# The steps at which a kernel prepares the next batch's softmax, set anew: both transposes in step 10, the state's read in step 12

## The chip, the cores and the metric

One Trainium2 chip, one of its cores. The metric is the device time of one execution in microseconds (us), the median of several runs; one further execution was taken with the hardware profiler, and all rows below are from it.

## The reference

The attention-like front end reads 8 batches of 512 tokens (8 heads of width 64) against 32 state vectors per head, in both directions, and two feed-forward layers follow on all 8 x 544 rows:

```python
scores = scale * np.matmul(x, state.transpose(0, 1, 3, 2))      # softmax over the 32 states
xread = np.matmul(a, state)
scores2 = scale * np.matmul(state, x.transpose(0, 1, 3, 2))     # softmax over the 512 tokens
sread = np.matmul(a2, x)
...
h = x @ w_in;  r = np.maximum(h, 0.0);  x = (s * (r * r) + b) @ w_out
h = x @ w_in;  g = h * (1.0 / (1.0 + np.exp(-h)));  out = g @ w_out
```

## The kernel before

All matrix products are of 32-bit accuracy: each operand is split into a high and a low part, and three products (high x high, high x low, low x high) are summed. For the first layer the states are folded into the first weights beforehand (the tiles `G`), so that its left operand is the softmax itself (`at_h`, `at_l`, the tiles `xh` and `xl`).

The first layer runs block by block. Block i (i = 1 to 7) is batch i; block 0 was done in a start-up part, and a last block holds the state rows. A block has 16 steps f. In `run`, one step issues in this order: the second half of the activation of step f-1 (`finish`: `gh` on ScalarE, L613, then `gl` on VectorE, L614), six matmuls of the first product (`mm1_a`, L566) into one of two banks `ph`, the activation's first half (relu on ScalarE, L607, then a square with scale on VectorE, L608), twelve matmuls of the second product of step f-3 (`mm2_a`, L628, which read `gh` and `gl` of step f-3), and then the extras of step f:

```python
do(f, 0)
finish()
pend.append((i, f, act_a(mm1_a(f, k), width[k], i)))
do(f, 1)
...
flush(LAG)          # LAG = 3
...
do(f, 2)
```

Every engine works through its queue in the order in which this code issues. The extras, kept by `extra(bi)` in a table of (step, place), are:

- the softmax of batch i+1, in two halves p and q (`Half`), in blocks 1 to 6. `score` (step 1) is on TensorE. Then for each half, in the order of the list `names`: `tr`, `rd`, `nb` (VectorE), `ex` (exp, ScalarE, gives `e2` and its sums); `mx`, `sb` (L470, L476, VectorE), `en` (exp, L481, ScalarE); `n0`, `n1` (tiny) and `n2` (L494, VectorE: `e2` times the reciprocal of its sum); `s0` to `s2` (L511 to L521), `s3` (L525), `s4` (L531), all on VectorE; `tu` (L503: four 128x128 transposes of `e2` on TensorE into a bank of the pool "a", which has two), `pl` (ScalarE, pulls that bank to `a2`); `ah` (ScalarE) and `al` (VectorE, L232), which make the `xh` and `xl` of the next block;
- `read` (L390, 64 small matmuls that read `a2` of both halves) and `pull_read` (L398); `load_all` of `xn`, the batch's rows that the next block's `read` needs (four loads on SyncE's DMA queue, L364);
- `split_g`, which splits the folded weights of later steps (a ScalarE copy, L229, and a VectorE subtraction, L232);
- conversions of the 64-bit weights for later: one ScalarE operation (L189) and four VectorE bit operations (L197 to L211) for each tile, sums of tiles (L750), reorders on ScalarE (L229).

```python
def n2(self, dve=True):
    ... nc.vector.tensor_scalar(out=self.e2, in0=self.e2, scalar1=self.rs, ...)
def tu(self, at="a"):
    self.pt = bank(at, [P, 4, P])
    for t in range(4):
        nc.tensor.transpose(self.pt[:, t, :], self.e2[:, t * P:(t + 1) * P], ident)
```

Of the kernel before, what the change touches and what calls it, by code (L numbers as in the profile page):

```python
# [87 lines left out]
def fused_kernel(ctx: ExitStack, tc, xt, xn, sbd, sg, w1, w2, sv, bv, out):  # L88
# [573 lines left out]
    def run(blocks, pend):  # L662
# [10 lines left out]
        for i, k in enumerate(blocks):  # L673
            if i == 0:
                continue
            ops = extra(i)

            def do(f, when):
                for op in ops.get((f, when), ()):
                    op()  # L680

            for f in range(NF):
# [4 lines that stand above are left out]
                last = f == NF - 1 and i + 1 == len(blocks)  # L687
                if last:
                    finish()
                flush(LAG)  # L690
                if f == NF - 1 and not last:
                    prepare_a(blocks[i + 1])
                if last:
                    flush(0)
                do(f, 2)
# [632 lines left out]
    def last_block(add):  # L1328

        def give(*tags):
            add(f, 2, spare.extend, tags)

        splits = [(p, c) for p in RIGHT for c in range(2)]
        inputs[0] = Inputs(0)
        for f in range(NF):
            if f == 0:
                give("xt0", "xt1", "xn0", "xn1", "sbd",
                     "xh2", "xh3", "xl2", "xl3", *(f"v{i}" for i in range(24, 30)),  # L1340
                     *(f"xr{i}" for i in range(4)))
                for i in range(2):
                    add(f, 2, carve, f"raw{i}", 4)
                add(f, 2, inputs[0].load)
            if f >= 2:
                give(f"wh{f - 2}", f"wl{f - 2}")
            if f == 7:
                give(*(f"mid{i}" for i in range(4)))
                give(*(f"v{i}" for i in range(8, 16)))
            if f == 11:  # L1350
                give(*(f"v{i}" for i in range(8)))
            if f == 15:
                give(*(f"v{i}" for i in range(16, 24)))
            if 2 <= f < 4:
                for name in ("T1", "T2", "T3"):
                    add(f, 2, inputs[0].sum, name, f - 2)
            for i, what in ((f - 4, inputs[0].high), (f - 5, inputs[0].low)):
                if 0 <= i < len(splits) // 2:
                    for p, c in splits[2 * i:2 * i + 2]:
                        add(f, 2, what, p, c)  # L1360
            for i, what in ((f - 6, "load"), (f - 9, "high"), (f - 10, "low")):
                if i >= 0 and i % 2 == 0 and i // 2 < 5:
                    if what == "load":
                        quads[i // 2] = list(duos_in(i // 2))
                    for x in quads[i // 2]:
                        add(f, 2, getattr(x, what))
# [53 lines left out]
    def extra(bi):  # L1420
        k = order[bi]
        ops = {}

        def add(f, when, op, *args):
            ops.setdefault((f, when), []).append(lambda: op(*args))

        if bi < B - 1:

            halves = [Half(k + 1, j) for j in range(2)]
            add(1, 2, score, k + 1, halves)  # L1430
            add(1, 2, load_sbd, k + 2)
            add(2, 0, load_all, k + 2, xt)
            names = "tr rd nb ex mx sb en n0 n1 n2 s0 s1 s2 s3 s4 tu pl ah al"
            when = (
                (1, 1, 1, 1, 3, 3, 3, 3, 3, 4, 5, 5, 5, 6, 6, 6, 6, 7, 8),
                (2, 2, 2, 2, 7, 7, 7, 7, 7, 8, 9, 9, 9, 10, 10, 9, 10, 11, 12),
            )
            for h, fs in zip(halves, when):
                for f, name in zip(fs, names.split()):
                    add(f, 2, getattr(h, name))  # L1440
            add(11, 2, read, k + 1, halves)
            add(12, 0, load_all, k + 2, xn)
            add(12, 2, pull_read, k + 1, halves)
        def add_g(f0, fs, *g):
            for j in range(2):
                add(f0, 0, load_g, *g, j)
                add(fs[j], 2, split_g, *g, j)

        if bi == 1:
            add_g(0, (1, 2), 1, 1)  # L1450
            add(2, 0, load_all, 2, xn)
        if bi < B:

            for fg, (f0, *fs) in enumerate(((1, 4, 4), (3, 6, 7), (9, 12, 13), (11, 14, 15))):
                if fg < 2:
                    g = k, fg + 2
                elif k + 1 < B:
                    g = k + 1, fg - 2
                else:
                    continue  # L1460
                add_g(f0, fs, *g)
        for f in range(NF):
            for when in range(3):
                for op in later.pop((NF * bi + f, when), ()):
                    add(f, when, op)
        if bi == B - 1:
            for i, pair in enumerate(stream[:2]):
                add(5 + 3 * i, 0, load32, pair)
            for i in range(RING // 2):
                add(9 + 2 * i, 2, split_next)  # L1470
        if bi == B:
            for f in (0, 1, 4, 5):
                add(f, 2, split_next)
            last_block(add)
        return ops
# [79 lines left out]
```

## Time and profile before

| what | us |
|---|---|
| median of 3 runs (lowest to highest) | 1343.88 (1342.68 to 1344.85) |
| the profiled execution | 1343.82 |
| its span, first to last instruction | 1342.0 |
| TensorE busy | 1309.4 |
| VectorE busy | 993.8 |
| ScalarE busy | 741.1 |
| blocks 1 to 6, the stretch that the change touches | about 137 to 550 |

"Busy" of TensorE is the union of its matmuls; a matmul's end in the trace is modelled. In a row of a timeline the first number is the start in us from the span's start, the second the duration, and a bracket at the end gives how long the engine stood idle before it and which instruction ended that.

### The profile page before, as it was taken

Reading aid. Unit: us, or ns where it says so; the run is one execution under the profiler, and the core shown is the slowest. Engines: PE = TensorE matmul, PEld = TensorE weight load, DVE = VectorE, ACT = ScalarE, POOL = GpSimd, SP = SyncE. Lnnn points to the kernel's source line nnn. Section 1 sums busy time; section 2 is a strip of 40 time slices with the busy share of each in tenths; the row PEclk is TensorE's granted clock in tenths of the full one; section 3 lists DMA queues with packets and bytes.
Section 4 is the critical chain, followed back from the end, with each engine's and each line's share of the span. In section 5 each row is a group of like instructions: output and inputs, shape, how many; then the busy total and the mean of one; then the engine's idle time right before and its main releaser. Section 6 shows DMA issues by size and latency. Waiting matters only on the chain.

```text
span 1342.0 us, 20852 instructions
## 1 busy us (share of the span) xinstructions
PE 1309.4 (98%) x6928; PEld 1133.0 (84%) x6928; DVE 993.8 (74%) x1794; ACT 741.1 (55%) x1360; POOL 0.7 (0%) x7
## 2 busy tenths in 40 slices
PE   5999999999999999999999999999999999999997
PEld 3678778787787777888988888999998888899997
DVE  8899797879797979865867757575767765655654
ACT  7999554444454545544665645464666635353541
POOL 0000000000000000000000000000000000000000
PEclk9999999999999999999999999999999999999999
DMA  8888555554565545343748565657699886677583
GB/s 304 304 304 287 190 189 196 171 182 143 172 203 180 179 160 180 127 151 90 231 150 290 205 226 212 234 191 242 210 297 351 304 262 189 179 238 228 168 259 88
DMA packets 182925, 284.01 MB, mean 212 GB/s; under 512 B 25632, under 2 KB 99360, under 8 KB 182816
## 3 DMA queue, kind: packets, MB, share of 16 engines
q1 hardware_dynamic: 182016, 282.28, 63.5%
q8 instruction: 54, 0.88, 0.3%
q10 hardware_dynamic: 800, 0.39, 0.1%
q14 instruction: 55, 0.45, 0.1%
HBM read 166.72 MB, written 115.87 MB: 211 GB/s over the span
## 4 chain that ended last, share of the span: by engine, by line
PE 79%; DVE 9%; DMA 6%; ACT 3%; issue 2%; SPq 1%; ACTq 0%; DVEq 0%
PE bank L902 48%; PE o L628 18%; PE ph L566 10%; DMA raw<-w 3%; DVE r L608 1%; DVE v L232 1%; DVE gl L614 1%; PE bank L281 1%; DMA v<-gd 1%; ACT wf L189 1%; DVE wf L206 1%; ACT xr L229 1%; DMA gd<-xr 1%; DMA x<-o 1%; SPq L327 0%
## 5 line engine op out<-in xcount | busy, mean ns | idle before, releaser
L566 PE MATMUL ph<-xh,v 128*128 128x512 f32 (+1 forms) x640 | 207.2, 375 | 0.1
L628 PE MATMUL o<-gh,wh 128*128 128x512 f32 (+1 forms) x448 | 169.9, 379 | 0.0
L628 PE MATMUL o<-gl,wh 128*128 128x512 f32 (+1 forms) x448 | 169.7, 379 | 0.0
L628 PE MATMUL o<-gh,wl 128*128 128x512 f32 (+1 forms) x448 | 169.7, 379 | 0.0
L566 PEld LDWEIGHTS ph<-xh,v 128*128 128x128 f32 x640 | 117.9, 190 | 27.0 <-issue 5.0
L608 DVE SCALAR_TENSOR_TENSOR r<-r,s_sb 128x512 f32<-128x512 f32 (+1 forms) x128 | 91.4, 714 | 49.9 <-ACT r L607 49.7
L607 ACT ACTIVATE r<-ph 128x512 f32<-128x512 f32 (+1 forms) x128 | 72.0, 563 | 94.6 <-PE ph L566 92.1
L566 PE MATMUL ph<-xl,v 128*128 128x512 f32 (+1 forms) x320 | 118.5, 370 | 0.0
L613 ACT ACTIVATE gh<-r,b_sb 128x512 fp32r<-128x512 f32 (+1 forms) x96 | 66.5, 693 | 57.7 <-DVE r L608 57.5
L628 PEld LDWEIGHTS o<-gh,wh 128*128 128x128 f32 x448 | 84.8, 189 | 15.8
L628 PEld LDWEIGHTS o<-gh,wl 128*128 128x128 f32 x448 | 84.6, 189 | 15.9
L628 PEld LDWEIGHTS o<-gl,wh 128*128 128x128 f32 x448 | 84.6, 189 | 15.7
L902 PE MATMUL bank<-v,v 128*128 128x384 f32 (+1 forms) x316 | 96.2, 360 | 0.0
L614 DVE SCALAR_TENSOR_TENSOR gl<-r,b_sb,gh 128x512 fp32r<-128x512 f32 (+1 forms) x96 | 68.5, 713 | 15.4 <-ACT gh L613 15.4
L902 PE MATMUL bank<-wh,v 128*128 128x384 f32 (+1 forms) x230 | 76.6, 352 | 0.0
L628 PE MATMUL o<-v,wh 128*128 128x512 f32 (+1 forms) x256 | 75.2, 377 | 0.0
L566 PEld LDWEIGHTS ph<-xl,v 128*128 128x128 f32 x320 | 60.7, 190 | 9.3
L902 PEld LDWEIGHTS bank<-v,v 128*128 128x128 f32 x316 | 58.6, 188 | 5.8
L628 PEld LDWEIGHTS o<-v,wh 128*128 128x128 f32 x256 | 46.9, 188 | 9.2 <-DVE o L641 0.5
L211 DVE SCALAR_TENSOR_TENSOR wf<-raw,wf 128x512 uint32<-128x512 uint32 (+1 forms) x65 | 52.9, 814 | 2.0
L902 PE MATMUL bank<-wl,v 128*128 128x384 f32 (+1 forms) x153 | 52.9, 357 | 0.4 <-DVE wh L750 0.4
L206 DVE SCALAR_TENSOR_TENSOR wf<-raw,wf 128x512 uint32<-128x512 uint32 (+1 forms) x65 | 52.2, 803 | 0.2
(1066 smaller groups left out, 3179.2 us busy)
## 6 DMA issues: line engine op xcount, KB each, us to landing
raw<-w SPq DMA_DIRECT2D x80, 512.0 KB, 4.9
gd<-xr SPq DMA_DIRECT2D x48, 256.0 KB, 2.9
v<-gd SPq DMA_DIRECT2D x192, 64.0 KB, 2.2
go<-v SPq DMA_DIRECT2D x54, 192.0 KB, 2.1
go<-v SPq DMA_DIRECT2D x38, 256.0 KB, 2.3
v<-go SPq DMA_DIRECT2D x45, 192.0 KB, 3.3
v<-go SPq DMA_DIRECT2D x31, 256.0 KB, 4.7
go<-wl SPq DMA_DIRECT2D x35, 192.0 KB, 2.1
```

The source lines that it names most:

```text
L189: nc.scalar.activation(out=tf, in_=hi.bitcast(F32), func=AF.Abs)
L206: nc.vector.scalar_tensor_tensor(out=t, in0=lo, scalar=29, in1=t, op0=ALU.logical_shift_right, op1=ALU.bitwise_or,)
L211: nc.vector.scalar_tensor_tensor(out=t, in0=hi, scalar=0xC0000000, in1=t, op0=ALU.bitwise_and, op1=ALU.bitwise_or,)
L229: nc.scalar.activation(out=out, in_=x, func=AF.Copy)
L232: nc.vector.tensor_tensor(out=lo, in0=x, in1=hi.bitcast(F32), op=ALU.subtract)
L566: nc.tensor.matmul(ph[:, :n], a, x, start=j == 0 and i == 0, stop=j == last and i == 2)
L607: nc.scalar.activation(out=r, in_=ph[:, :n], func=AF.Relu)
L608: nc.vector.scalar_tensor_tensor(out=r, in0=r, scalar=s_sb, in1=r, op0=ALU.mult, op1=ALU.mult)
L613: nc.scalar.activation(out=gh, in_=r, func=AF.Identity, bias=b_sb)
L614: nc.vector.scalar_tensor_tensor(out=gl, in0=r, scalar=b_sb, in1=gh.bitcast(F32), op0=ALU.add, op1=ALU.subtract)
L628: nc.tensor.matmul(po[c][:, :n], a, x, start=f == 0 and i == 0, stop=f == NF - 1 and i == 2)
L902: nc.tensor.matmul(bank[:, :n], a, x, start=start and j == 0 and i == 0, stop=stop and j == last and i == 2, skip_group_check=True,)
```

## The change

In the table `when` of `extra`, each half has a row of 19 steps, one for each name of the list `names`. Half p's `s0` to `s4`, `ah`, `tu` and `pl` come later, half q's `mx`, `sb`, `en`, `n0`, `n1` come earlier (from step 7 to 5), and q's `tu` and `pl` one step later. `read`, `pull_read` and the `xn` loads move by one step. Nothing is added or removed.

```diff
             names = "tr rd nb ex mx sb en n0 n1 n2 s0 s1 s2 s3 s4 tu pl ah al"
             when = (
-                (1, 1, 1, 1, 3, 3, 3, 3, 3, 4, 5, 5, 5, 6, 6, 6, 6, 7, 8),
-                (2, 2, 2, 2, 7, 7, 7, 7, 7, 8, 9, 9, 9, 10, 10, 9, 10, 11, 12),
+                (1, 1, 1, 1, 3, 3, 3, 3, 3, 4, 6, 6, 6, 7, 7, 10, 11, 8, 8),
+                (2, 2, 2, 2, 5, 5, 5, 5, 5, 8, 9, 9, 9, 10, 10, 10, 11, 11, 12),
             )
...
-            add(11, 2, read, k + 1, halves)
-            add(12, 0, load_all, k + 2, xn)
-            add(12, 2, pull_read, k + 1, halves)
+            add(12, 2, read, k + 1, halves)
+            add(13, 0, load_all, k + 2, xn)
+            add(13, 2, pull_read, k + 1, halves)
```

TensorE, block 1, the end of step 6 and the start of step 7 (`mid_1719` is half p's `e2`; lines with - are of before, with + of the change):

```order
 L628 MATMUL o_1824<-gl_1809,wh_897 128x512
 L628 MATMUL o_1824<-gh_1808,wl_908 128x512
-L503 MATMUL bank<-ident,mid_1719 128x128 x4
 L566 MATMUL ph<-xh_1152,v_1722 128x512
 L566 MATMUL ph<-xl_1471,v_1722 128x512
```

The transposes of half p leave step 6 and nothing takes their place. Now the place that they go to, the end of step 10 of the same block (`mid_1787` is half q's `e2`):

```order
+L628 MATMUL o_1824<-gl_1962,wh_1207 128x512
+L628 MATMUL o_1824<-gh_1961,wl_1224 128x512
+L503 MATMUL bank<-ident,mid_1719 128x128 x4
 L503 MATMUL bank<-ident,mid_1787 128x128 x4
 L566 MATMUL ph<-xh_1152,v_1866 128x512
```

Both halves' transposes now stand in one place, behind the second product of step 7 (its `gh` and `gl` have the numbers 1961 and 1962); half q's stood there behind step 9's matmuls, one step earlier.

VectorE, block 1, from step 5's square (`r_1885`) on, before (`mid_1714` and `mid_1782` are the scores `sn` of p and q, `gl_1887` is `gl` of step 5):

```order
L608 SCALAR_TENSOR_TENSOR r_1885<-r_1885,s_sb 128x512
L511 TENSOR_REDUCE sm<-mid_1714 128x16
L516 TENSOR_SCALAR sm<-sm 128x16
L521 RECIPROCAL sm<-sm 128x16
L197 TENSOR_SCALAR wf_1792<-wf_1792 128x512
L201 TENSOR_SCALAR wf_1792<-wf_1792 128x512
L614 SCALAR_TENSOR_TENSOR gl_1887<-r_1885,b_sb,gh_1886 128x512
L608 SCALAR_TENSOR_TENSOR r_1917<-r_1917,s_sb 128x512
L525 TENSOR_TENSOR mid_1714<-mid_1714,sm 128x512
L531 STREAM_TRANSPOSE v_1935<-mid_1714 128x512
```

and from the same instruction on in the changed kernel:

```order
L608 SCALAR_TENSOR_TENSOR r_1885<-r_1885,s_sb 128x512
L470 TENSOR_REDUCE mx<-mid_1782 128x16
L476 TENSOR_TENSOR mid_1782<-mid_1782,mx 128x512
L485 TENSOR_SCALAR sum_1788<-sum_1788 128x1
L490 RECIPROCAL sum_1788<-sum_1788 128x1
L197 TENSOR_SCALAR wf_1792<-wf_1792 128x512
L201 TENSOR_SCALAR wf_1792<-wf_1792 128x512
L614 SCALAR_TENSOR_TENSOR gl_1887<-r_1885,b_sb,gh_1886 128x512
L608 SCALAR_TENSOR_TENSOR r_1919<-r_1919,s_sb 128x512
L511 TENSOR_REDUCE sm<-mid_1714 128x16
L516 TENSOR_SCALAR sm<-sm 128x16
L521 RECIPROCAL sm<-sm 128x16
```

Half q's four operations take the place of p's three, and p's move one step back each; from step 8 on both orders have had the same instructions.

ScalarE, block 1, from step 5's relu (`r_1885`) on, before:

```order
L607 ACTIVATE r_1885<-ph 128x512
L613 ACTIVATE gh_1886<-r_1885,b_sb 128x512
L607 ACTIVATE r_1917<-ph 128x512
L229 ACTIVATE mid_1942<-bank 128x512
L229 ACTIVATE v_1944<-v_1794 128x512
L189 ACTIVATE wf_1953<-raw_1836 128x1024
L613 ACTIVATE gh_1918<-r_1917,b_sb 128x512
L607 ACTIVATE r_1964<-ph 128x512
L229 ACTIVATE xh_1981<-v_1935 128x512
L481 ACTIVATE mid_1782<-mid_1782 128x512
L229 ACTIVATE v_1946<-v_1796 128x512
L613 ACTIVATE gh_1965<-r_1964,b_sb 128x512
```

and in the changed kernel:

```order
L607 ACTIVATE r_1885<-ph 128x512
L481 ACTIVATE mid_1782<-mid_1782 128x512
L613 ACTIVATE gh_1886<-r_1885,b_sb 128x512
L607 ACTIVATE r_1919<-ph 128x512
L229 ACTIVATE v_1940<-v_1794 128x512
L189 ACTIVATE wf_1949<-raw_1836 128x1024
L613 ACTIVATE gh_1920<-r_1919,b_sb 128x512
L607 ACTIVATE r_1960<-ph 128x512
L229 ACTIVATE v_1942<-v_1796 128x512
L613 ACTIVATE gh_1961<-r_1960,b_sb 128x512
```

Half q's exponential (L481) moves from behind step 7's relu to behind step 5's, and half p's pull (`mid_1942`) and `xh` leave these steps.

## Rows read from the trace of the kernel before

**Rows 1.** The page's first part: busy us, share, instructions.
```profile
PE 1309.4 (98%) x6928; PEld 1133.0 (84%) x6928; DVE 993.8 (74%) x1794; ACT 741.1 (55%) x1360; POOL 0.7 (0%) x7
```
**Rows 2.** Waits of TensorE from 137 to 641 us: us, times, longest.
```profile
PE bank L503 <- DVE mid L494: 8.5, 6, 2.7
```
**Rows 3.** Timeline of TensorE, the transposes of half q, blocks 1 to 6.
```profile
178.47 0.63 PE L503 MATMUL bank<-ident,mid 128*128 128x128 f32 x4 [0.72 <-DVE mid L494]
...
249.79 0.63 PE L503 MATMUL bank<-ident,mid 128*128 128x128 f32 x4 [2.38 <-DVE mid L494]
...
323.03 1.09 PE L503 MATMUL bank<-ident,mid 128*128 128x128 f32 x4 [2.67 <-DVE mid L494]
...
394.00 0.63 PE L503 MATMUL bank<-ident,mid 128*128 128x128 f32 x4 [0.56 <-DVE mid L494]
...
464.09 0.63 PE L503 MATMUL bank<-ident,mid 128*128 128x128 f32 x4 [1.02 <-DVE mid L494]
...
534.29 0.63 PE L503 MATMUL bank<-ident,mid 128*128 128x128 f32 x4 [1.12 <-DVE mid L494]
```
**Rows 4.** Timeline of TensorE: block 3, first matmuls of steps, half p's transposes.
```profile
303.39 0.39 PE L566 MATMUL ph<-xh,v 128*128 128x512 f32 x1
...
307.47 0.60 PE L503 MATMUL bank<-ident,mid 128*128 128x128 f32 x4
307.83 0.48 PE L566 MATMUL ph<-xh,v 128*128 128x512 f32 x1
...
312.04 0.39 PE L566 MATMUL ph<-xh,v 128*128 128x512 f32 x1
...
316.12 0.39 PE L566 MATMUL ph<-xh,v 128*128 128x512 f32 x1
...
323.77 0.78 PE L566 MATMUL ph<-xh,v 128*128 128x512 f32 x1
...
329.08 0.39 PE L566 MATMUL ph<-xh,v 128*128 128x512 f32 x1
```
**Rows 5.** The same in block 2, first matmuls of steps 10 and 11.
```profile
250.18 0.47 PE L566 MATMUL ph<-xh,v 128*128 128x512 f32 x1
...
255.98 0.39 PE L566 MATMUL ph<-xh,v 128*128 128x512 f32 x1
```
**Rows 6.** Busy time by stretch: us, PE, PEld, DVE, ACT, POOL, PEclk, DMA, GB/s.
```profile
324.00:325.00 1.00, 1.00 (x4) 0.81 (x4) 1.00 (x3) 0.00 (x0) 0.00 (x0) 0.50 1.00 401
```
**Rows 7.** Instructions of line 503: duration in ns, least, median, most.
```profile
L503 PE MATMUL bank<-ident,mid x60: 270/272/448, 33.7 to 534.6; 128*128 128x128 f32 x60
```
**Rows 8.** Timeline of VectorE, block 3, steps 5 to 10.
```profile
306.73 0.68 DVE L511 TENSOR_REDUCE sm<-mid 128x16 f32<-128x512 f32 x1
...
315.93 0.68 DVE L470 TENSOR_REDUCE mx<-mid 128x16 f32<-128x512 f32 x1
...
317.43 0.16 DVE L490 RECIPROCAL sum<-sum 128x1 f32<-128x1 f32 x1
318.55 0.69 DVE L232 TENSOR_TENSOR v<-v,v 128x512 fp32r<-128x512 f32 x1 [0.96 <-DMA v<-gd]
...
320.48 0.75 DVE L614 SCALAR_TENSOR_TENSOR gl<-r,b_sb,gh 128x512 fp32r<-128x512 f32 x1
...
322.41 0.48 DVE L494 TENSOR_SCALAR mid<-mid,sum 128x512 f32<-128x512 f32 x1
...
327.95 0.75 DVE L608 SCALAR_TENSOR_TENSOR r<-r,s_sb 128x512 f32<-128x512 f32 x1
```
**Rows 9.** Timeline of ScalarE, block 3, steps 5 to 7.
```profile
306.84 0.72 ACT L613 ACTIVATE gh<-r,b_sb 128x512 fp32r<-128x512 f32 x1 [2.06 <-DVE r L608]
307.47 0.58 ACT L607 ACTIVATE r<-ph 128x512 f32<-128x512 f32 x1
308.11 0.60 ACT L229 ACTIVATE mid<-bank 128x512 f32<-128x512 f32 x1
...
317.36 0.63 ACT L481 ACTIVATE mid<-mid 128x512 f32<-128x512 f32 x1 [4.05 <-DVE mid L476]
```

## Prediction

> **What bounds the kernel now.** I read the page's first part first. TensorE is busy for 1309.4 of 1342.0 us, VectorE for 993.8, ScalarE for 741.1 [rows 1]: the time is TensorE's own work plus its pauses, so a change that adds and removes no matmul can only act through pauses. The list of TensorE's waits comes next. In the stretch of the first layer's blocks it has one line: the transposes of line 503 wait for line 494, the scaling `n2` of the same tile, six times, 8.5 us in all [rows 2]. The timeline says which ones: always half q's, once a block, with 0.56 to 2.67 us of idle time before them [rows 3]. Half p's transposes stand in the timeline without a bracket, that is, without a wait [rows 4].
>
> A wait costs more than its idle time, for two reasons.
> - A step without a visit by other work takes 316.12 - 312.04 = 4.08 us for its 18 matmuls, so a matmul is followed by the next after 0.227 us, but its row ends 0.39 us after its start [rows 4]. The idle time is counted from that end, so each wait costs 0.16 us more than its bracket says.
> - In blocks 2 and 3, where TensorE stood for 2.38 and 2.67 us, it went on at half its clock: the granted clock of 324 to 325 us is 0.50, that is 1.2 GHz in place of 2.4 [rows 6]. Step 10 took 255.98 - 250.18 = 5.80 us in block 2 [rows 5] and 329.08 - 323.77 = 5.31 us in block 3; a step behind a visit without a wait takes 312.04 - 307.83 = 4.21 [rows 4]. That is 1.59 and 1.10 us more. Block 3's transposes themselves took 323.77 - 323.03 = 0.74 us up to the next matmul where half p's took 0.36 [rows 3, 4]: 0.38 more.
>
> **Why half q is late.** VectorE is behind in these steps. In block 3 step 5's square ends and step 5's extras begin at 306.73; from there VectorE runs without a pause until `n1` of half q ends at about 317.5, then stands for 0.96 us before the subtraction of `split_g` at 318.55 [rows 8]. The row names a DMA, but the ScalarE copy that feeds this subtraction is queued behind half q's exponential, which waited until 317.36 for `sb` [rows 9]; I take that as the cause. So `gl` of step 7 starts at 320.48 and `n2` of half q at 322.41, ending at 322.89, just ahead of the transposes at 323.03 [rows 3, 8].
>
> **The change, part by part.** I give block 3, the one with the longest wait, in the times of before.
>
> 1. *Half p's transposes leave step 6.* Their visit cost 0.36 us up to the next matmul (307.47 to 307.83) and 0.13 in the step behind (4.21 against 4.08), 0.49 together [rows 4]. Steps 8, 9 and 10 so begin 0.49 earlier: 311.55, 315.63 and 319.71.
>
> 2. *Both transposes come at the end of step 10*, at 319.71 + 4.08 = 323.79. VectorE's instructions up to `n2` of half q are the same ones as before, only permuted, so without any gain it ends at 322.89, 0.9 us ahead. If the pause of 1.04 us (317.51 to 318.55) goes, since no exponential stands ahead of that copy any more, `n2` ends at 321.85, 1.9 us ahead. Either way no wait remains. That takes out 8.47 us of idle time (the six brackets of [rows 3]), 6 x 0.16 = 0.98 us of matmul ends, and 1.59 + 1.10 + 0.38 = 3.07 us of half clock: **12.5 us**.
>
> 3. *One visit in place of two.* Four transposes of 0.27 us each [rows 7] take 0.60 in all [rows 4], so they start (0.60 - 0.27) / 3 = 0.11 apart; four cost 0.44 of a visit's 0.49, and joining saves 0.05 a block, 0.3 us. The bounds are nothing at all (if the second four need all their 0.49) and 6 x 0.13 = 0.8 us (if the effect on the step behind is paid once). I take 0.3, from the rows' own spacing.
>
> 4. *Half q's exponential moves to step 5, ahead of `gh` of step 5 and relu of step 6 on ScalarE.* Its cover is the two banks `ph`: step 8's first product needs relu of step 6 done, at 311.55. `mx` of q starts at 306.73, and the exponential came 317.36 - 315.93 = 1.43 us behind it [rows 8, 9], so it runs from 308.16 to 308.79; `gh` takes 0.63 and relu 0.58 [rows 9], which ends at 310.0. 1.5 us are left; a copy in between, at the 0.60 of a pull [rows 9], leaves 0.9. Cost nothing. What it gives: `gh` and relu of steps 7 and 8 are no longer stuck behind an exponential that ScalarE met in step 7 and stood before for 4.05 us [rows 9].
>
> 5. *The activation must keep up with a TensorE that no longer pauses.* Step 10's second product needs `gl` of step 7 six matmuls into the step, at 319.71 + 1.36 = 321.07. Before, `gl` was done at 320.48 + 0.75 = 321.23; with the pause gone at 320.19, with 0.9 us to spare. If the pause stays, this costs 0.2 us in block 3. This is the narrowest place that I find.
>
> 6. *Both pulls in step 11, `read` in step 12.* Queued on ScalarE in step 11 are `gh` of step 10, relu, and then the two pulls. `gh` waits for the square of step 10, before at 327.95 [rows 8], now at 326.91, done at 327.66. With 0.63, 0.58 and 2 x 0.60 the second pull ends at 330.1. `read` comes after step 12: step 11 begins 0.36 + 0.44 after 323.79, and two steps of 4.21 and 4.08 lead to 332.9. 2.8 us are left. `pull_read` and the `xn` loads move along behind `read`, the loads at the same distance as before on SyncE's queue; the next reader of `xn` is a block away. Half p's `ah` and `al` now meet in step 8; their product is needed in the next block.
>
> The sum is 1343.82 - 12.5 - 0.3 = **1331.0 us**. The profiled execution (1343.82) and the median (1343.88) agree, so the same time stands for both.
>
> **Rivals.**
> - *A wait remains in front of step 8 or step 10.* If VectorE reaches `sb` of q later than above, the exponential in step 5 holds up relu of step 6, and step 8 waits; or `gl` of step 7 is late. For it speaks that the margins are 1.5 and 0.9 us in a queue that is full; against it, that the order shows the same VectorE work. From the margin on each us costs one us a block: one us over in all six blocks, with 0.16 each, gives 1331 + 7 = 1338.
> - *The wait moves along, no change.* It would be so if the transposes waited for their bank of the pool "a", which has two tiles and no more after the change, and where two are now filled back to back. The six releasers are all line 494, which writes `e2`, and none is a reader of a bank [rows 2, 3]. Time 1343.8. The Trainium skill, "Perfetto Trace Analysis", section "Optimization Strategy", says that consistent bubbles, the same gap repeating on the engine that should be saturated, can mean that there isn't enough SBUF or PSUM for the next tile; by that rule this rival is right, but the trace names another releaser all six times, and the measurement decides.
> - *Slower.* `read` now stands one step behind two pulls, where before half p's was long done. If the second pull ends 2.8 us later than I walk it, TensorE waits there instead, and a stop as long as block 3's 2.67 us with 0.16 and its half clock (1.10 + 0.38) costs 4.3 us a block: 1331 + 26 = 1357. It passes the time before when each block loses over 12.8 / 6 = 2.1 us there. Against it: VectorE has no new work and ScalarE is at 55%.
>
> **How the numbers follow.** A measurement of this kernel tells 0.2%, 2.7 us, from no change. My forecast, all six waits gone and none in their place, has a chance of 0.78 (1330.5 to 1333 by the bounds above). The remaining wait has 0.11, the unchanged time 0.05, the slower case 0.06. The first two are both faster than 1341.2: faster 0.89, the same 0.05, slower 0.06. The range goes from 1329.4 (12.5 and 0.8 us gone, less the 1.1 us by which the runs spread) to 1335.5, which takes in the smaller half of the remaining waits.
>
> **What would show it.** No row of line 503 with a bracket; no half clock between 137 and 540 us; step 10 with its visit, from its first matmul to step 11's, at 4.08 + 0.36 + 0.44 = 4.88 us in all six blocks, and step 6 at 4.08. The forecast is wrong if line 566 or 628 waits in steps 8 to 10, or line 390 in step 12, or if VectorE's pause of step 7 comes back in steps 5 and 6.

## The result: 0.9903 of the time before

The changed kernel takes 1329.94 us (median of 4, 1329.01 to 1331.01) against 1343.28 for the kernel before on the same chip (median of 4, 1340.72 to 1344.85). The ratio is 0.9903, with a 95% interval of 0.9885 to 0.992 that lies clear of 1: the kernel is 13.3 us faster. 1331.0 us was forecast.

The page of the changed kernel begins so (busy us, share, instructions):

```profile
span 1328.3 us, 20847 instructions
## 1 busy us (share of the span) xinstructions
PE 1304.9 (98%) x6928; PEld 1131.6 (85%) x6928; DVE 993.1 (75%) x1794; ACT 739.1 (56%) x1360; POOL 0.7 (0%) x7
```

TensorE's list of waits for the blocks, one line before [rows 2], is empty now. The busy time of the whole stretch says the same in one row (us, then PE, PEld, DVE, ACT, POOL, granted clock, DMA share, GB/s):

```profile
137.00:629.00 492.00, 492.00 (x2643) 401.82 (x2642) 409.63 (x752) 246.73 (x418) 0.00 (x0) 1.00 0.52 173
```

TensorE is busy for all 492 us, at full clock: it has no pause left there. The timeline of TensorE in block 3 (the first matmuls of steps 8 to 12, the transposes at the end of step 10 and the read at the end of step 12) answers to [rows 4] and to the third of [rows 3]:

```profile
304.95 0.39 PE L566 MATMUL ph<-xh,v 128*128 128x512 f32 x1
...
309.04 0.39 PE L566 MATMUL ph<-xh,v 128*128 128x512 f32 x1
...
313.12 0.39 PE L566 MATMUL ph<-xh,v 128*128 128x512 f32 x1
...
317.20 1.03 PE L503 MATMUL bank<-ident,mid 128*128 128x128 f32 x8
317.99 0.48 PE L566 MATMUL ph<-xh,v 128*128 128x512 f32 x1
...
322.17 0.39 PE L566 MATMUL ph<-xh,v 128*128 128x512 f32 x1
...
326.34 0.43 PE L390 MATMUL bank<-xn,mid 128*32 128x64 f32 x16
```

The eight transposes stand in one row without a bracket. Step 10 with all eight takes 317.99 - 313.12 = 4.87 us (4.88 was forecast); before, step 9 of block 3 with half q's four took 323.77 - 316.12 = 7.65. The step behind takes 4.18, at full clock. It is the same in all six blocks, within 0.01 us.

To compare runs I use one stretch of the timeline, from the first matmul of block 1's step 2 to the first matmul of step 1 of the state rows, and call it **the blocks' stretch**. It holds all that the change touches, and not the start-up or the second layer: the stretch begins 142.4 to 145.0 us into the ten profiled executions of this document, and the kernel before alone has 142.5 and 143.8 among them. In the kernel before it goes from 143.82 to 629.98, 486.16 us; now from 142.43 to 615.54, **473.11 us: 13.05 us less**. The span fell by 13.7: the start-up happened to be 1.4 us shorter, and the part behind the stretch 0.7 longer.

### The profile page after: what moved, and what is told of

Read it like the earlier page. It is cut to its first block, busy times and chain, and to the rows that moved or that the text cites. A ratio compares the mean times of both kernels' runs of the same rounds, so it can differ in the third digit from the quotient of the medians.

```text
span 1328.3 us, 20847 instructions
## 1 busy us (share of the span) xinstructions
PE 1304.9 (98%) x6928; PEld 1131.6 (85%) x6928; DVE 993.1 (75%) x1794; ACT 739.1 (56%) x1360; POOL 0.7 (0%) x7
## 4 chain that ended last, share of the span: by engine, by line
PE 92%; DMA 2%; DVE 2%; ACT 2%; issue 1%; SPq 0%; ACTq 0%
PE bank L902 48%; PE o L628 26%; PE ph L566 15%; DMA raw<-w 1%; PE bank L281 1%; ACT xr L229 1%; DMA gd<-xr 1%; DMA v<-sums_O 0%; PE bank L390 0%; PE bank L377 0%; PE bank L503 0%; DVE v L232 0%; DVE wf L211 0%; ACT wf L189 0%; DVE wl L232 0%
```

## The experiments

Theory A is the prediction's: the transposes of half q waited because their `n2` ended late, and one more step is enough. Theory B, its rival here: the place of half q's exponential in ScalarE's queue made the waits, and the transposes' own step is secondary. The first two kernels are the two halves of the change, each alone; the third has half p's transposes in a place of their own again. Each stretch below is from one profiled execution. In the diffs a line with - is the changed kernel's.

**Half q's transposes one step later, nothing else** but the pull, the read and the `xn` loads that go with them.

```diff
-                (1, 1, 1, 1, 3, 3, 3, 3, 3, 4, 6, 6, 6, 7, 7, 10, 11, 8, 8),
-                (2, 2, 2, 2, 5, 5, 5, 5, 5, 8, 9, 9, 9, 10, 10, 10, 11, 11, 12),
+                (1, 1, 1, 1, 3, 3, 3, 3, 3, 4, 5, 5, 5, 6, 6, 6, 6, 7, 8),
+                (2, 2, 2, 2, 7, 7, 7, 7, 7, 8, 9, 9, 9, 10, 10, 10, 11, 11, 12),
```

> Only half q's transposes and pull go one step later (steps 10 and 11), with the read and the xn loads one step later; the softmax steps and half p's transposes stand as before. Theory A (the transposes waited because n2 ended 0.6 to 2.7 us after step 9, so one step of 4.08 us is enough): all six waits on n2 go, 12.5 us; a rest of about 0.45 + 0.16 us remains in blocks 2 and 3 each, since relu of step 8 there ended at 247.7 and 320.65, with step 10 due at 247.25 and 320.20. Ratio to before about 0.9915 (-11.3 us). Theory B (the waits went because half q's exponential no longer blocks ScalarE in step 7): the queue is as late as before and the wait turns up at line 566 or 628 in steps 10 and 11, with most of its size; ratio 0.998 to 1.0.

Measured: ratio 0.993 (0.9911 to 0.9948), which is 9.3 us less than before where 11.3 were expected, with the expected 0.9915 inside the interval. The blocks' stretch is 474.85 us: 11.31 less than in the first profile of the kernel before, from which the 11.3 were worked out, but only 9.7 to 9.8 less than in its two later ones, which had less half clock (end of this section). The waits that are left stand where they were expected, in the timeline of TensorE at the first matmul of step 10 of blocks 2 and 3:

```profile
248.01 0.50 PE L566 MATMUL ph<-xh,v 128*128 128x512 f32 x1 [0.37 <-ACT r L607]
...
317.41 0.50 PE L566 MATMUL ph<-xh,v 128*128 128x512 f32 x1 [0.35 <-ACT r L607]
```

TensorE now waits for a relu, and ScalarE's timeline of block 3 shows that it is the relu behind the copy, the conversion and `gh`, all queued behind the exponential:

```profile
314.62 0.61 ACT L229 ACTIVATE v<-v 128x512 fp32r<-128x512 f32 x1
315.14 1.12 ACT L189 ACTIVATE wf<-raw 128x1024 f32<-128x1024 f32 x1
316.17 0.71 ACT L613 ACTIVATE gh<-r,b_sb 128x512 fp32r<-128x512 f32 x1
316.79 0.57 ACT L607 ACTIVATE r<-ph 128x512 f32<-128x512 f32 x1
```

VectorE's pause in step 7 is there as well (the bracket names the ScalarE copy behind the exponential), 0.95 or 0.96 us in each of the six blocks as before:

```profile
315.27 0.69 DVE L232 TENSOR_TENSOR v<-v,v 128x512 fp32r<-128x512 f32 x1 [0.95 <-ACT v L229]
```

So the queues are as late as they were, and the later step alone still takes out all six waits on `n2`: theory B falls as the main cause. But two small waits show behind them.

**The softmax steps spread anew, the transposes apart at steps 6 and 9.**

```diff
-                (1, 1, 1, 1, 3, 3, 3, 3, 3, 4, 6, 6, 6, 7, 7, 10, 11, 8, 8),
-                (2, 2, 2, 2, 5, 5, 5, 5, 5, 8, 9, 9, 9, 10, 10, 10, 11, 11, 12),
+                (1, 1, 1, 1, 3, 3, 3, 3, 3, 4, 6, 6, 6, 7, 7, 6, 6, 8, 8),
+                (2, 2, 2, 2, 5, 5, 5, 5, 5, 8, 9, 9, 9, 10, 10, 9, 10, 11, 12),
...
-            add(12, 2, read, k + 1, halves)
+            add(11, 2, read, k + 1, halves)
```

(and the `xn` loads and `pull_read` at step 12).

> Only the softmax steps are spread anew (half q's mx to n1 at step 5, half p's s0 to s4 and ah one step later); the transposes stay apart at steps 6 and 9, the pulls at 6 and 10, the read at 11. Theory A: n2 of half q ends where it ends in the changed kernel, which is 0.50, 0.60, 2.58, 0.46, 1.39 and 0.68 us after step 9 of blocks 1 to 6; half p's visit puts TensorE 0.49 later, so waits of about 0, 0.1, 2.1, 0, 0.9 and 0.2 us remain, 3.3 us with 0.16 for each on top, and perhaps 1.5 us of half clock in block 3: 4 to 6 us of the 12.5 stay, ratio 0.9935 to 0.995. Theory B: the waits go, ratio 0.990 to 0.991.

Measured: ratio 0.9968 (0.9953 to 0.9982), with the whole interval above the expected 0.9935 to 0.995. The blocks' stretch is 478.32 us, 7.84 less than in the first profile of before, so 4.7 of the 12.5 us stay, inside the expected 4 to 6. Against the two later profiles of before it is only 6.2 to 6.4 less, which accounts for 1.5 us of the miss. The rest seems to lie outside the blocks, in parts that the change does not touch: they took 856.7 us in this profile and 853.9 to 855.8 in the three of before. Three brackets remain, in blocks 3, 5 and 6:

```profile
317.84 0.63 PE L503 MATMUL bank<-ident,mid 128*128 128x128 f32 x4 [2.11 <-DVE mid L494]
...
456.73 0.63 PE L503 MATMUL bank<-ident,mid 128*128 128x128 f32 x4 [0.87 <-DVE mid L494]
...
526.39 0.63 PE L503 MATMUL bank<-ident,mid 128*128 128x128 f32 x4 [0.57 <-DVE mid L494]
```

VectorE's pause in step 7 is gone from all six blocks, and block 3's wait is 2.11 us in place of 2.67. The two halves of the change overlap: 11.3 and 7.8 us alone and 13.05 together, all against the first profile of before. By theory B the new spread alone would have taken all the waits out, so it fails here too. The later step does most, the new spread clears what would have shown behind it.

**The transposes apart again, all else as changed.**

```diff
-                (1, 1, 1, 1, 3, 3, 3, 3, 3, 4, 6, 6, 6, 7, 7, 10, 11, 8, 8),
+                (1, 1, 1, 1, 3, 3, 3, 3, 3, 4, 6, 6, 6, 7, 7, 6, 6, 8, 8),
```

> The changed kernel with half p's transposes and pull back at step 6, all else as in the changed kernel. Theory A: no waits; two visits of 0.49 us each in place of one of 0.89 a block (step 10 with its visit took 4.87 in place of 4.08, the step behind 4.18), so 0.1 us a block, 0.5 us in all: ratio to the changed kernel 1.000 to 1.001, ratio to before 0.9905 to 0.991. Rival (joining the visits is what pays): clearly slower than the changed kernel, by 3 us or more.

Measured: ratio to before 0.9921 (0.9906 to 0.9937); no wait; the blocks' stretch is 473.49 us, 0.38 more than the changed kernel's. Joining the visits is worth 0.4 us of the 13. The time by itself could not tell that; the stretch can, since each of the six blocks is longer, by 0.03 to 0.09 us.

**Transposes done twice.** The price of a transpose by itself (the second four write the same bank again).

```diff
-            for t in range(4):
+            for t in [*range(4)] * (2 if self.b > 1 else 1):
                 nc.tensor.transpose(self.pt[:, t, :], self.e2[:, t * P:(t + 1) * P], ident)
```

> The changed kernel with each half's four transposes done twice into the same bank (48 more in blocks 1 to 6). Theory A (a transpose costs 0.11 us behind another, a visit 0.05 to 0.1 on top): step 10 with its visit goes from 4.87 to 4.87 + 0.88 = 5.75 us, no wait appears, 5.3 us in all. Rival (each transpose costs its row's 0.27 us): 13 us.

Measured: 1336.18 us in one execution; step 10 with its visit takes 5.75 us in every block, and the blocks' stretch is 478.37 us, 5.26 more than the changed kernel's. TensorE in block 1:

```profile
181.99 1.91 PE L503 MATMUL bank<-ident,mid 128*128 128x128 f32 x16
183.66 0.48 PE L566 MATMUL ph<-xh,v 128*128 128x512 f32 x1
```

Sixteen transposes take 183.66 - 181.99 = 1.67 us up to the next matmul where eight took 0.79: 0.88 us for eight more, 0.11 each, not the 0.27 of their rows: in the trace a transpose's row ends after the next one has started.

**The read one step earlier, behind the pulls of its own step.** The rival on the slower side, brought about here.

```diff
-            add(12, 2, read, k + 1, halves)
-            add(13, 0, load_all, k + 2, xn)
-            add(13, 2, pull_read, k + 1, halves)
+            add(11, 2, read, k + 1, halves)
+            add(12, 0, load_all, k + 2, xn)
+            add(12, 2, pull_read, k + 1, halves)
```

> The changed kernel with the read one step earlier, at 11, behind the pulls of the same step, and the xn loads and pull_read one step earlier as well. In the changed kernel the second pull ends 1.02, 1.03 and 1.56 us after the end of step 11 in blocks 1 to 3, 0.57 ahead of it in block 4, and 1.03 and 0.32 after it in blocks 5 and 6. Theory A: TensorE waits at line 390 for a pull, 5.0 us in all, no half clock (the longest is 1.6 us): 1335 us, ratio to before about 0.994. Rival (the read is covered anyhow): as the changed kernel, 1330.

Measured: ratio 0.9956 (0.994 to 0.9973), 1336.0 us; the blocks' stretch is 478.04, 4.93 more than the changed kernel's, against the 5.0 expected. The six blocks are longer by 1.02, 1.00, 1.58, 0.00, 1.01 and 0.32 us, nearly what the expectation has for each; the brackets of line 390 hold only 3.1 us of that. TensorE, then ScalarE, in block 3:

```profile
327.29 0.30 PE L390 MATMUL bank<-xn,mid 128*32 128x64 f32 x2 [0.98 <-ACT mid L229]
327.78 0.37 PE L390 MATMUL bank<-xn,mid 128*32 128x64 f32 x11 [0.19 <-ACT mid L229]
```

```profile
325.55 0.72 ACT L613 ACTIVATE gh<-r,b_sb 128x512 fp32r<-128x512 f32 x1 [2.48 <-DVE r L608]
326.18 0.58 ACT L607 ACTIVATE r<-ph 128x512 f32<-128x512 f32 x1
326.65 1.07 ACT L229 ACTIVATE mid<-bank 128x512 f32<-128x512 f32 x2
```

The read stops for the first pull, then for the second. ScalarE itself had waited 2.48 us for VectorE's square before the `gh` ahead of them, and in the other blocks 0.69 to 3.15: the pulls are late because VectorE is, and not because ScalarE has too much to do. So the read's move to step 12 is needed: without it the change gives back 4.9 us.

**Half q's transposes in the step of their `n2`.** A stop made longer, for the price of a stop.

```diff
-                (2, 2, 2, 2, 5, 5, 5, 5, 5, 8, 9, 9, 9, 10, 10, 10, 11, 11, 12),
+                (2, 2, 2, 2, 5, 5, 5, 5, 5, 8, 9, 9, 9, 10, 10, 8, 11, 11, 12),
```

> The changed kernel with half q's transposes at step 8, the step that issues their n2, and half p's alone at step 10. Theory A: TensorE waits until n2 ends; in the changed kernel that is 4.6, 4.7, 6.7, 4.5, 5.5 and 4.8 us behind the end of step 8, 30.7 us in all, and each of these stops, all longer than the 2.4 and 2.7 us after which the kernel before went on at half clock, brings half clock for 1.1 to 1.6 us of loss: 1330 + 31 + 8 = 1369 us, ratio to before 1.019. Rival (only the stop itself counts): 1361, ratio 1.013.

Measured: ratio 1.0238 (1.0218 to 1.0259), 1374.04 us, above both expectations. The stops were the expected ones, 30.66 us in the six brackets:

```profile
177.82 1.09 PE L503 MATMUL bank<-ident,mid 128*128 128x128 f32 x4 [4.57 <-DVE mid L494]
...
330.65 1.09 PE L503 MATMUL bank<-ident,mid 128*128 128x128 f32 x4 [6.67 <-DVE mid L494]
```

The stretch is 515.98 us, 42.87 more than the changed kernel's. 30.66 us are idle time, 6 x 0.16 = 1.0 the matmul ends, 0.4 the second visit; 10.8 us are left, 1.8 a block on average, for half clock. It follows every one of these stops: the granted clock of the 3 us behind each is 0.50 to 0.58. The step behind the stop takes 5.2 to 6.3 us in place of 4.2. In block 1, from 178 to 181 us:

```profile
178.00:181.00 3.00, 3.00 (x10) 2.52 (x10) 2.39 (x5) 0.00 (x0) 0.00 (x0) 0.50 0.33 117
```

I had expected 8 us for the half clock, and nothing for the matmul ends and the second visit. The mechanism held, its size was too small.

**The kernel before, twice more.** In the profiled execution of before both long stops were followed by half clock; is that regular?

> The kernel before once more, for its half clock. If the half clock behind the stops of 2.4 and 2.7 us in blocks 2 and 3 is regular, the stretch from block 1's step 2 to the state rows' first step is 486 us again. If it comes in some executions only, that stretch is 1 to 3 us shorter with the same idle times in the brackets.

> As the run before it: a third execution of the kernel before, to see whether half clock follows the stops of blocks 2 and 3 each time (stretch 486 us) or not (483 to 485 us).

Measured: 1340.42 and 1340.40 us; the blocks' stretches are 484.68 and 484.51 us, 1.5 and 1.65 less than in the first profile, with the same brackets (8.4 and 8.5 us in all). The granted clock behind block 2's stop and behind block 3's, first in the one execution (stops of 2.41 and 2.67 us), then in the other (2.40 and 2.67):

```profile
249.00:252.00 3.00, 3.00 (x9) 2.40 (x8) 2.93 (x7) 0.68 (x2) 0.00 (x0) 0.50 0.82 218
322.00:325.00 3.00, 3.00 (x17) 2.51 (x16) 2.93 (x7) 1.26 (x3) 0.00 (x0) 1.00 0.94 343
```

```profile
249.00:252.00 3.00, 3.00 (x16) 2.52 (x15) 2.97 (x6) 0.55 (x1) 0.00 (x0) 1.00 0.81 222
321.00:323.00 2.00, 2.00 (x7) 1.61 (x6) 1.97 (x4) 0.72 (x1) 0.00 (x0) 0.50 0.98 388
```

Half clock followed one stop only in each, once that of block 2 and once that of block 3. So the 3.07 us that the prediction took from one execution are about 1.5 in the two others.

The blocks' stretch of all kernels, in us:

| kernel | from | to | stretch | against the changed one |
|---|---|---|---|---|
| before, first profile | 143.82 | 629.98 | 486.16 | +13.05 |
| before, second and third | 142.53, 142.64 | 627.21, 627.15 | 484.68, 484.51 | +11.57, +11.40 |
| changed | 142.43 | 615.54 | 473.11 | |
| only q's transposes later | 144.95 | 619.80 | 474.85 | +1.74 |
| only the spread | 143.75 | 622.07 | 478.32 | +5.21 |
| transposes apart | 143.77 | 617.26 | 473.49 | +0.38 |
| read at step 11 | 144.39 | 622.43 | 478.04 | +4.93 |
| transposes twice | 144.59 | 622.96 | 478.37 | +5.26 |
| q's transposes at step 8 | 143.87 | 659.85 | 515.98 | +42.87 |

No variant here beats the changed kernel, whose TensorE has no pause left in the blocks.

## Why the prediction was right

1. *Half p's visit leaves step 6.* Right: steps 6 to 9 take 4.07 to 4.09 us each in block 3, and no trace of a visit is left.
2. *The waits go because the transposes come one step later.* Right, and shown by itself: with that step alone, the old spread and VectorE's old pause, all six brackets go, as "either way no wait remains" has it. The margin in block 3 was put at 1.9 us; it is 317.20 - 315.70 = 1.5, with `n2` from 315.22 to 315.70 (VectorE, block 3):

```profile
306.64 0.69 DVE L232 TENSOR_TENSOR v<-v,v 128x512 fp32r<-128x512 f32 x1 [0.31 <-ACT r L607]
...
313.29 0.74 DVE L614 SCALAR_TENSOR_TENSOR gl<-r,b_sb,gh 128x512 fp32r<-128x512 f32 x1
...
315.22 0.48 DVE L494 TENSOR_SCALAR mid<-mid,sum 128x512 f32<-128x512 f32 x1
```

The pause of step 7 is gone, as taken, in all six blocks. That the exponential made it, which the prediction took without a test, the runs now bear out: the pause stays in the run that leaves the exponential in step 7, and goes in those that move it to step 5. But it was 0.96 us by its bracket, not the 1.04 that the prediction subtracts, and in block 3 a pause of 0.31 us in step 6, which I had not seen, took a part of it back. Together these are 0.39 of the 0.44 us that are lacking in the margin. What the pause in step 6 waited for these rows don't settle.

3. *One visit in place of two: 0.3 us, at most 0.8.* 0.38 by the experiment, so in the bounds. That a transpose costs 0.11 us behind another is shown by the doubled ones.
4. *The exponential in step 5 costs nothing.* Right, and the margin is about the one worked out, 1.5 us: relu of step 6 ends at 303.31 (ScalarE, block 3), step 8 begins at 304.95, 1.6 later.

```profile
301.57 0.63 ACT L481 ACTIVATE mid<-mid 128x512 f32<-128x512 f32 x1 [3.40 <-DVE mid L476]
302.11 0.71 ACT L613 ACTIVATE gh<-r,b_sb 128x512 fp32r<-128x512 f32 x1
302.73 0.58 ACT L607 ACTIVATE r<-ph 128x512 f32<-128x512 f32 x1
...
322.65 1.08 ACT L229 ACTIVATE mid<-bank 128x512 f32<-128x512 f32 x2
```

What I undervalued is its use. I named it in passing, and costed only `gl` of step 7 in case the old pause stayed, at 0.2 us in block 3. The experiment with the old places shows the wait at relu of step 8 instead, 0.37 and 0.35 us of idle time in blocks 2 and 3. The rows for it were there: ScalarE's queue behind half q's exponential.

5. *The activation keeps up.* Right, and it is the narrowest of the places worked out: `gl` of step 7 ends at 314.03, and the second product of step 10 begins at 313.12 + 1.36 = 314.48. 0.45 us are left where I worked out 0.9, for the reasons of point 2.
6. *Both pulls in step 11, read in step 12.* Right: the pulls end at 323.73, the read comes at 326.34, 2.6 us later (2.8 worked out). With the read in step 11 the rival on the slower side appears, at 4.9 us in all.

Of the rivals, the remaining wait and the return of the wait elsewhere did not come about: no bracket stands in the blocks. A gap that repeats on the engine that should be busy can, by the Trainium skill ("Perfetto Trace Analysis", "Optimization Strategy"), mean too few buffers. Here it did not: with the same two banks all six waits on `n2` go when only the step changes.

The forecast of 1331.0 against 1329.94 hides one term that was too large as an expectation: the half clock. Taken from one execution, it was 3.07 us; in two others it is about 1.5. The time forecast does not hang on this: what the first profile had of half clock stands in the time that the sum starts from, and the sum takes the same off. The gain does. Against the two other executions the change gains 11.4 to 11.6 us in the blocks (8.5 of idle time, 1.0 of matmul ends, 0.4 by joining, about 1.5 of half clock), and 13.05 only against the first, where 12.8 was forecast. The difference of the medians, 13.3 us, is that of the runs shown and has an interval of about 2.4 us to each side. On the chips of the later runs the kernel before had a median of 1341.77 and 1342.27 us in place of 1343.28, so it is partly luck that the measured gain came so near the forecast one.

## What to carry to other kernels

Where the engine that bounds a kernel stops in the same place of each round, look at when the releaser ends against the next place where the waiting work could stand: here 0.6 to 2.7 us late against a step of 4.08 us, so one step later was enough, and its own user had to move along. Before a stop is taken out, look at what it covered: read off, in the queues beside it, what will be needed earlier by as much as the stop was long; here that was a relu 0.4 us late behind an exponential, and spreading the work anew cleared it. And price a stop from more than one execution when the clock is part of it.

## What the runs showed of the hardware

The granted clock did not fall after each stop of the same length. After stops of 2.38 to 2.67 us in blocks 2 and 3 it was half in four of six cases, in three executions of the same kernel; after 2.11 us (the spread alone, block 3) it stayed full; after each of the six stops of 4.5 to 6.7 us it was half, and that cost 1.3 to 2.4 us a stop beyond the idle time, 1.8 on average. What decides between half and full after the stops of 2.4 to 2.7 us stays open.
